# Counting ranks on VectorE with a second masked comparison, and a ReLU wait per step

## The chip, the core and the metric

The kernel runs on one core of one Trainium2 chip. Five engines work side by side, each through its own list of instructions in order: TensorE (matmuls, called PE in the profile, with its weight loads PEld), VectorE (DVE), ScalarE (ACT), GpSimd (POOL), and SyncE (SP), which mostly issues transfers. They wait for each other by semaphores. TensorE writes its results to PSUM, eight banks of 512 float32 values on each of 128 partitions; everything else lies in SBUF. The metric is the device time of one execution in microseconds (us), and each kernel is given by the median of several runs.

## The reference

Two blocks follow each other. The first is a cross attention for 8 batches and 8 heads: 512 rows of `x` (64 wide) read from 32 state rows, and the state rows read from `x`. Both results are put together to 544 rows, and the heads side by side give 512 columns. The second block scores each row, takes the 128 rows with the highest score in each batch, sends them through two layers, and adds the result, weighted by a sigmoid of the score, to those rows alone:

```
xread = softmax(scale * x @ state.T) @ state        # 512 rows
sread = softmax(scale * state @ x.T) @ x            # 32 rows
x2    = concat(xread, sread), heads side by side     # 544 x 512 for each batch
scores[b] = x2[b] @ w_gate
top = the 128 rows with the highest score
h  = relu(x2[b, top] @ w1)                          # 512 -> 1024
ye = h @ w2                                         # 1024 -> 512
out[b] = x2[b];  out[b, top] = x2[b, top] + sigmoid(scores[b, top]) * ye
```

All values are float32.

## The kernel before

The kernel is written as small steps, called pieces, each bound to one engine: `add("PE", "scores", ...)` makes one and names what it must follow and which buffers it takes and uses. Nothing is issued while the pieces are made. At the end `carry_out` (lines 145 to 163) issues them in the order of a list of numbers, `ORDER` (lines 18 to 44). This one list sets the order on every engine and queue, SP's and POOL's among them. An entry such as `663/3/w03` also names the PSUM bank that the piece takes (3), and `w03` puts three warm-up matmuls, whose result nobody reads, into bank 0 ahead of it. If the list doesn't hold every piece's number exactly once, the pieces are issued in the order in which they were made. The text calls a piece by its name and its batch, as in `scores.4`; for the two layers the number is that of the group.

**Attention, one batch at a time (lines 390 to 622).** `x` is loaded in two or four transfers (`load_x`). For batches 0 to 3 TensorE turns it (`turn`) and ScalarE copies it out (`turned`). For batches 4 to 7 a second, rearranged load (`load_x2`, four transfers, one buffer in all) comes in and VectorE turns blocks of it (`blocks`, L405). `scores` (L438) fills two PSUM banks. On VectorE follow `in` (a turn, L457), `max`, `sub`, `sum` and `mult` (the softmax along the state) and `out` (a turn back, L486), with `exp` on ScalarE between them; `smax` and the two `sexp` make the other softmax. `read` (two halves, L549) makes the 512 rows and, in an extra column, their scores by head; `gate` (VectorE, L557) adds these up and `rows` (ScalarE, L553) copies the rows out. For batches 4 to 7 the second softmax's weights are turned by `blocks_a` (VectorE), a transfer to DRAM `a_out` and four transfers back `a_in`; `sread` (L611) then makes the 32 state rows, `srows` scales them. `store_x` and `store_s` write the rows to the output.

**Choice, one batch at a time (lines 664 to 829).** The 544 scores lie in `sc` as five columns: four with 128 partitions, one with 32. `gate_s`, `heads` and `score_s` make the last column. `row` and `row_s` (TensorE) with `row_kept` and `row_s_kept` (ScalarE) spread all scores as one row over every partition, `srow`. A row's rank is the number of rows that beat it. Column `c` of the table `after` masks the places behind the own one, so `win` (L725, five VectorE instructions) compares each score of column `c` with all scores from column `c` on, keeps only the places behind its own, and sums along the row (`over`). It leaves the 0/1 matrix in the buffers `win0` to `win4`. The wins over rows ahead are not computed again: the piece `over` (L751, 15 matmuls with a column of ones) sums those matrices along the other direction. `off` (L757, L758) subtracts the two counts. `oh` (L762) turns the result to a one-hot matrix of 128 slots, `pick` (L778) multiplies it by row numbers and scores (kept by `parts`, POOL, in three bfloat16 parts), `index` makes the row numbers as integers, and `fetch` (POOL) gathers the chosen rows from the output. `below`, `exps`, `plus`, `inverse` and `sigmoid` make the weight.

**Layers, for groups of batches (lines 831 to 928).** The groups are [0], [1, 2], [3, 4], [5, 6] and [7], numbered 0 to 4. `xg` turns the fetched rows, eight pieces `first` (L886) make the first layer, `relu` (L889) copies it out in two or four steps, and `second` (L906; four pieces of two blocks each) makes the second layer for each batch; for batches 6 and 7 it is made in two halves of the columns, `second_h`. `add` or `add_h` (L909) weights and adds, `put` (POOL) scatters the rows to the output. Each `second` piece waits for all `relu` pieces of its group.

Of the kernel before, what the change touches and what calls it, by code (L numbers as in the profile page):

```python
# [15 lines left out]


ORDER = """
0 1 2 4 17 3 6 7 8 9 18 19 10 11 30/5/w08 32/4 34/0/w01 36/1 26/7 31 5 35 27 33 37 12 38/0/w23 113/6 39 13 14 115/5
24/7 40/0 117/4 44 15 114 25 116 45 118 46 28/6 41 16 119/2 62/3 178/4 64/7 180/5 42 120 43 29 63 65 21 23 20 53 487  # L20
182/1 184/6 121/2 267/7 66/0 47 48 122 185 181 268 183 179 67 126 123 49/1 269/4 51/6 50 270 127 128 52 174/4 141/7
54/0 271/5 124 330 55 70 142 125 56 57 272 175 273/7 71/6 58/0 274 129 132 72 59 130 131 176/4 73/5 143/6 75/7 61 177
74 60 76 68 144 69 82 186/4 485/7 133/0 145/6 80 81 79 187 134 188 78 77 191 486 135 136 146 137/0 275/6 140 139 192
193 149 138 280 83/1 208/5/w01 150/2 84 85 151 197 86/3 206/2 152/1 154/0 88 276 189 209 207 87 153 155 281 282 89 22
161 90 210/3 295/2/w01 328/0 297/6 95/7 159 158 160 157 156 333 331 148 147 336 162/1 190 96 329 296 298 211 194 163
195 277 196 278 164 214 97/5 98 102/7 103 99 100 198/0 165/4 215/6 104 199 167 168 335 213 334 279 200 201 101 91
202/0 105 216 283 286 203 284 285 217/5 219/6 226 92 204 106 218 166 220 205 107/7 287/3 239/2 222 221 223 225 224
227/0 108 240 289 290 93 228 229 288 230/5 291/0 299/6 232 292 109 306/4 294 231 300 293 307 337 339 303 340 338 304/6
341/0 305 346 212 332 169 233 315 94 234 308/2 241/6 309 242 347 348 170 313 311 310 314 312 110 243/3 316/6 361 362
342 317 343 318 344 301 302 424 422 426 363 427 425 246/4 249/0 319/1 252/5 250 244 253 247 320 345 245 235 321 111  # L30
349 352 350 431 351 429 428 430 322 364 251 254 353/0 394/5 365/7 354 248 355 356 366 395 357/0 369 370/6 358 371 171
323 112 381 236 372/5 374/4 373 375 359 360 378 380 377 379 376 261/7 255/5 382/2 432/3 256 262 423 490 493 488 368
367 492 491 383 437 384 385/0 263 257 264 258 438 439 237 452 453 387 433 434 496 497 435 172 495 443 494 454 238 388
173 455 396/6 498/2 436 397 398/4 399 456/1 401/6 440 503 259 499 441 504 457 324 505 386 400 442 518 519 460 500 265
589 590 591 459 592 520 489 521 402 444/0 461/5 445 501 446 502 447 404/7 405 407/4 448/0 408 462 506 594 507 509 449
593 508 596 595 472 325 389 406 403 450 451 409 463/5 510/0 465/4 410/6 522/7 464 512 466 513 523 470 511 326 467 468
471 469 526 514/2 473/1 527/7 515 528 474 475 517 516 458 524 587 525 529/0 531/7 530 532 390 535 533 534 537 536
597/4 476/2 411 539/7 327 538 266 391 478 602 540 392 541 412 542/1 603 604 543 477 544 598 617 618 599 600 479 545
260 546 393 480 413 416/2 417 418 551/5 553/4 419 619 588 620 601 552 554 605 420 606 607 608 414 555/7 561/4 558/5
609/0 621/6 556 559 547 611 622 557 612 625 610 613/0 626/6 627 614 481 615 616 482 548 637 421 624 623 562 628/2  # L40
630/1 564/0 629 631 560 563 634 632 633 636 635 565 638/3 566 639 640 549 567/4 641/1 581/3 568 574/6 582 569 575 583
576 584 577 642 645 550 646 580 647 643 578 483 585 648 644 649 669 484 573 579 586 415 662 650/5 651 570 652/0 653
654 655 657/6 658 659 660 656 661 663/3/w03 664 665 666 670/5 671 672 673 571 667 668 572 674 675
"""


# [1 line left out]
def kernel(  # L48
# [10 lines left out]
    nc = tc.nc  # L59
# [24 lines left out]
    def pool(name, bufs, **kw):  # L84
        return ctx.enter_context(tc.tile_pool(name=name, bufs=bufs, **kw))
# [9 lines left out]
    GATES_PE = (0, 2)  # L95
    WIDE = (0, 1, 2, 3)
    ROWS_OUT = ()
    const = pool("const", 1)
    xin = pool("xin", N_X)
    work = pool("work", 1)  # L100
# [121 lines left out]
    wg_h = const.tile([H, D], F32, name="wg_h")  # L222
    wg_T = const.tile([D, H], F32, name="wg_T")
    after = const.tile([128, SP], F32, name="after")
    places = const.tile([128, NC + 1, n_slots], F32, name="places")
    ones = const.tile([128, 1], BF16, name="ones")
    same_n = const.tile([128, Ns], F32, name="same_n")
# [18 lines left out]
    def pool_tables():  # L246

        nc.gpsimd.iota(num[:, 0, :, 0:NC], pattern=[[SP, B], [1, NC]], base=0, channel_multiplier=NC)
        nc.gpsimd.iota(num[:, 0, :, NC], pattern=[[SP, B]], base=S, channel_multiplier=1)
        nc.gpsimd.iota(after, pattern=[[1, SP]], base=0, channel_multiplier=-1, allow_small_or_imprecise_dtypes=True)  # L250
        nc.gpsimd.tensor_scalar(after, after, 0.0, None, op0=ALU.is_gt)

        nc.gpsimd.iota(places, pattern=[[-128, NC + 1], [1, n_slots]], base=0, channel_multiplier=-1,
                       allow_small_or_imprecise_dtypes=True)
        nc.gpsimd.memset(ones, 1.0)

        nc.gpsimd.memset(sc, 0.0)
        for off in offs:  # L260
            nc.gpsimd.memset(off, 0.0)

    def row_numbers():

# [62 lines left out]
    p_w1 = load("SP", "load_w1", lambda: nc.sync.dma_start(out=w1, in_=moe_w1.rearrange("(j p) f -> p j f", p=128)))  # L327
    p_w2 = load("SP", "load_w2", lambda: nc.sync.dma_start(out=w2, in_=moe_w2.rearrange("(j p) m -> p j m", p=128)))
    p_tab = add("POOL", "tables", pool_tables, b=0)
    p_num = add("DVE", "numbers", row_numbers, after=[p_tab], b=0)  # L330
    p_t0 = add("DVE", "twice", lambda: twice(0, N_ST, nc.vector), after=[p_st0], uses=[stb], b=0)
    p_t = add("POOL", "twice", lambda: twice(N_ST, B, nc.gpsimd), after=[p_st], uses=[stb], b=0)
# [331 lines left out]
    def choice(b, tmp, p_sc, p_xt, p_st1):  # L664
# [60 lines left out]
            nc.vector.scalar_tensor_tensor(wins[c].ap[0:n], srow.ap[0:n, f:SP], sc[0:n, b, c:c + 1], after[0:n, 0:SP - f],  # L725
                                           op0=ALU.is_gt, op1=ALU.mult, accum_out=tmp["over"][0:n, c:c + 1])

        p_w = []
        for c in range(NC + 1):
            p_w.append(add("DVE", "win", lambda c=c: win(c), after=[p_r1, p_r2], takes=[wins[c]], uses=[srow], b=b))  # L730

# [22 lines left out]
        def offsets():  # L754
# [76 lines left out]
    def layers(units, number):  # L831
# [41 lines left out]
        p_h = []  # L873
# [23 lines left out]
        for u, lo in zip(units, at):  # L897
# [3 lines left out]
            for k, part in enumerate(parts):  # L901
# [81 lines left out]
```

## Time and profile before

| | |
|---|---|
| median of 3 runs | 204.92 us |
| lowest and highest run | 204.24 and 207.49 us |
| the profiled execution: its own time | 206.27 us |
| the profiled execution: span from first to last instruction | 204.5 us |
| TensorE busy | 192.0 us |
| VectorE busy | 127.7 us |
| ScalarE busy | 77.6 us |
| GpSimd busy | 51.8 us |
| mean granted TensorE clock | 0.981 |

The profile comes from one execution, so that its durations add up to its own time and not to the median. A line of groups names the line, engine, operation, what is written from what, the shape and the number of instructions; then come the total busy time in us, the mean of one in ns, and the idle time before them with what ended it. The granted clock is the share of full speed that TensorE was given. "L751" is line 751 of the kernel.

### The profile page before, as it was taken

Reading aid. Unit: us, or ns where it says so; the run is one execution under the profiler, and the core shown is the slowest. Engines: PE = TensorE matmul, PEld = TensorE weight load, DVE = VectorE, ACT = ScalarE, POOL = GpSimd, SP = SyncE. Lnnn points to the kernel's source line nnn. Section 1 sums busy time; section 2 is a strip of 40 time slices with the busy share of each in tenths; the row PEclk is TensorE's granted clock in tenths of the full one; section 3 lists DMA queues with packets and bytes.
Section 4 is the critical chain, followed back from the end, with each engine's and each line's share of the span. In section 5 each row is a group of like instructions: output and inputs, shape, how many; then the busy total and the mean of one; then the engine's idle time right before and its main releaser. Section 6 shows DMA issues by size and latency. Waiting matters only on the chain.

```text
span 204.5 us, 5844 instructions
## 1 busy us (share of the span) xinstructions
PE 192.0 (94%) x2474; PEld 139.9 (68%) x2474; DVE 127.7 (62%) x293; ACT 77.6 (38%) x178; POOL 51.8 (25%) x147
## 2 busy tenths in 40 slices
PE   7899888899999999899999999799999999999990
PEld 3587666689757688665448887644478886679980
DVE  4279999999966896745899878584764142010100
ACT  2389996682733512371132456312221351011100
POOL 8020030370532307010200004170810032305132
PEclk9999999999999999999999999859999999999999
DMA  6998975059894899979979968085680060101102
GB/s 194 342 273 301 409 274 197 5 113 325 155 305 147 234 263 175 222 127 334 201 135 136 192 159 256 8 260 167 209 193 10 19 258 0 51 0 42 64 26 77
DMA packets 67218, 35.04 MB, mean 171 GB/s; under 512 B 54904, under 2 KB 63096, under 8 KB 66168
## 3 DMA queue, kind: packets, MB, share of 16 engines
q1 hardware_dynamic: 64676, 28.97, 54.8%
q0 software_dynamic: 1312, 4.20, 6.6%
q10 hardware_dynamic: 1204, 1.51, 2.1%
q8 instruction: 19, 0.31, 0.7%
q14 instruction: 7, 0.06, 0.1%
HBM read 21.56 MB, written 13.11 MB: 170 GB/s over the span
## 4 chain that ended last, share of the span: by engine, by line
PE 57%; DVE 8%; DMA 8%; issue 6%; SPq 1%; POOLq 1%; ACT 0%; POOL 0%; DVEq 0%
PE ps L906 24%; PE ps L886 19%; DMA x<-in_x_dram 4%; PE ps L549 4%; DMA xr<-out_dram,idx 2%; PE ps L438 2%; DVE win L725 2%; PE ps L611 2%; PE ps L751 2%; PE ps L690 1%; DVE xT L405 1%; DMA out_dram<-ot,half 1%; PE ps L845 1%; DVE e L457 1%; PE ps L778 1%
## 5 line engine op out<-in xcount | busy, mean ns | idle before, releaser
L906 PE MATMUL ps<-w,hT 128*128 128x512 f32 (+1 forms) x160 | 60.3, 525 | 0.1
L886 PE MATMUL ps<-xg,w 128*128 128x256 f32 (+1 forms) x320 | 59.4, 341 | 0.0
L886 PEld LDWEIGHTS ps<-xg,w 128*128 128x128 f32 x320 | 50.4, 191 | 6.7 <-issue 1.4
L906 PEld LDWEIGHTS ps<-w,hT 128*128 128x128 f32 x160 | 29.7, 193 | 19.4 <-issue 17.2
L553 ACT COPY xs<-ps 128x512 f32<-128x512 f32 x32 | 17.8, 590 | 22.2 <-DVE sc L557 14.1
L909 DVE SCALAR_TENSOR_TENSOR ot<-ps,z,xr 128x512 f32<-128x512 f32 (+1 forms) x10 | 6.4, 639 | 26.6 <-PE ps L906 20.2
L725 DVE SCALAR_TENSOR_TENSOR win<-srow,sc,after 128x160 bf16<-128x160 f32 (+4 forms) x40 | 18.4, 511 | 5.4 <-ACT srow L716 5.4
L549 PE MATMUL ps<-st_v,eT 32*64 32x65 f32 (+1 forms) x768 | 16.6, 246 | 3.1 <-ACT xs L553 1.4
L549 PEld LDWEIGHTS ps<-st_v,eT 32*64 32x64 f32 (+1 forms) x768 | 14.3, 149 | 7.0 <-issue 4.6
L656 POOL DMA_INDIRECT xr<-out_dram,idx x8 | 8.5, 1066 | 38.6 <-DVE idx L782 25.1
L889 ACT ACTIVATE hT<-ps 128x512 f32<-128x512 f32 x16 | 9.4, 602 | 18.2 <-PE ps L886 18.2
L735 POOL CAST aux<-sc 128x5 bf16<-128x5 f32 x8 | 2.9, 356 | 46.7 <-DVE sc L557 32.6
L474 ACT ACTIVATE e<-e 128x1024 f32<-128x1024 f32 x8 | 8.5, 1064 | 15.8 <-DVE e L471 15.8
L496 ACT ACTIVATE a<-ps,nm 128x512 f32<-128x512 f32 x14 | 9.5, 689 | 12.9 <-DVE nm L492 9.2
L405 DVE STREAM_TRANSPOSE xT<-x 128x512 f32<-128x512 f32 x16 | 10.5, 683 | 2.8 <-DMA x<-in_x_dram 2.8
L478 DVE TENSOR_REDUCE sm<-e 128x32 f32<-128x1024 f32 x8 | 9.7, 1208 | 2.6 <-ACT e L474 2.6
L848 ACT COPY xg<-ps 128x512 f32<-128x512 f32 x8 | 4.6, 586 | 15.7 <-PE ps L845 15.7
L401 PE MATMUL ps<-ident,xf 128*128 128x128 f32 x64 | 9.8, 289 | 0.5 <-DMA xf<-in_x_dram 0.5
L438 PE MATMUL ps<-xT,st_T 64*32 64x256 f32 x256 | 9.8, 413 | 0.0
L483 DVE TENSOR_TENSOR e<-e,sm 128x1024 f32<-128x1024 f32 x8 | 9.7, 1207 | 0.0
L418 ACT COPY xT<-ps 128x512 f32<-128x512 f32 x14 | 7.9, 592 | 4.5 <-PE ps L401 4.5
L492 DVE TENSOR_REDUCE nm<-ps 128x2 f32<-128x1024 f32 x7 | 8.5, 1213 | 1.7 <-PE ps L693 1.0
(107 smaller groups left out, 242.6 us busy)
## 6 DMA issues: line engine op xcount, KB each, us to landing
xf<-in_x_dram SPq DMA_DIRECT2D x14, 512.0 KB, 7.1
out_dram<-xs SPq DMA_DIRECT2D x7, 1024.0 KB
w<-in_moe_w_dram SPq DMA_DIRECT2D x2, 2048.0 KB, 14.7
x<-in_x_dram SPq DMA_DIRECT2D x16, 256.0 KB, 8.6
a_d<-spare SPq DMA_DIRECT2D x4, 512.0 KB
aT<-a_d SPq DMA_DIRECT2D x16, 128.0 KB, 3.4
out_dram<-xs ACTq DMA_DIRECT2D x1, 1024.0 KB
xf<-in_x_dram SPq DMA_DIRECT2D x3, 256.0 KB
```

What stands on the lines that cost most here:

```text
L401: nc.tensor.transpose(v[:, k, r], xf[b].ap[:, 2 * pair + k, 2 * r:2 * r + 2].rearrange("p w d -> p (w d)"), ident)
L405: nc.vector.transpose(out=t.ap.rearrange("p k r t -> p r k t"), in_=x2[b].ap[:, :, 2 * pair:2 * pair + 2].rearrange("p r k s d -> p r k (s ...
L438: nc.tensor.matmul(view_s(False)[Ns * q:Ns * (q + 1), w, g], st_T[half, b, g, Ns * q:Ns * (q + 1)], xT[2 * g + q // 2].ap[half, q % 2].rea ...
L478: nc.vector.reduce_sum(out=sm, in_=e.ap, axis=AX.X)
L483: nc.vector.tensor_tensor(out=e.ap, in0=e.ap, in1=tmp["sm"].to_broadcast([128, 32, Ns]), op=ALU.mult)
L496: nc.scalar.activation(out=a.ap[:, g], in_=view_s()[:, :, g], func=AF.Exp, bias=tmp["nm"][:, g:g + 1], accum_out=tmp["ss"][:, g:g + 1])
L549: nc.tensor.matmul(view(o)[t, q, c - c0, g], eT.ap[r, c % 2, g, c // 2, t], st_v[r, b, g], start=True, stop=True)
L553: nc.scalar.copy(out=xs.ap[:, c].rearrange("p (g q m) -> p g q m", g=2, q=4), in_=view(o)[:, :, c - c0, :, 0:D].rearrange("p q g m -> p g ...
L725: nc.vector.scalar_tensor_tensor(wins[c].ap[0:n], srow.ap[0:n, f:SP], sc[0:n, b, c:c + 1], after[0:n, 0:SP - f], op0=ALU.is_gt, op1=ALU.mu ...
L886: nc.tensor.matmul(o, w(j), i[:, :, j] if n == 256 else i[:, 0, j], start=(j == 0), stop=(j == ND - 1))
L889: nc.scalar.activation(out=hT.ap[:, f0:f0 + nf, 0:n], in_=ph.ap.rearrange("p (f s) -> p f s", f=nf)[:, :, 0:n], func=AF.Relu)
L906: nc.tensor.matmul(py.ap[0:m, part], hT.ap[:, f, lo:lo + m], w2[:, f, part], start=(f == 0), stop=(f == NF - 1))
```

## The change

There are two edits, and a new order.

For batches 3 to 7 (`FULL`) a second set of five comparisons, `low`, is made on VectorE. It compares each score of column `c` with all scores up to the end of that column, takes "less than", masks by a new table `before`, and sums along the row (`under`). `before` holds ones for all columns ahead and, for the own column, zero at the own place and behind. GpSimd makes it once, with three operations. The piece `over` with its 15 matmuls is not made for these batches, and `off` subtracts `under` from `over`, both in SBUF. All five `low` write their unneeded 0/1 matrix into the buffer `win0`. Batches 0 to 2 are as before.

In the layers, a `second` piece for the blocks `f0` and `f0 + 1` waits for the ReLU pieces up to the one that makes these blocks, and no more for the later ones.

`ORDER` is replaced as a whole: 697 numbers in place of 676. The order of pieces on all engines and queues, the banks and the warm-ups (30 in place of 17) differ. On TensorE the three warm-ups before the last `second_h.4` are gone, `state_T.0` is ahead of the last two `turn.0`, both `xg.1` stand behind `row_s.3`, and two `second_h.3` stand ahead of the last `first.3`. On VectorE `out.4` stands ahead of the four `blocks.5`, and the `low` are interleaved with the `win`. On POOL `before` stands behind `below.0` and ahead of `parts.1`, and `fetch.1` behind `parts.2`. On SP `a_out.4` has three `load_x2.5` and a `load_x.5` ahead of it, and `a_in.4` one `load_x2.5` and `store_s.3` between.

```diff
+    FULL = (3, 4, 5, 6, 7)
...
+    before = const.tile([128, S + 128], BF16, name="before") if FULL else None
...
+    def pool_before():
+
+        nc.gpsimd.memset(before[:, 0:S], 1.0)
+        nc.gpsimd.tensor_tensor(out=before[:, S:S + 128], in0=after[:, 0:128], in1=ident, op=ALU.add)
+        nc.gpsimd.tensor_scalar(before[:, S:S + 128], before[:, S:S + 128], -1.0, 1.0, op0=ALU.mult, op1=ALU.add)
...
+    p_bef = add("POOL", "before", pool_before, after=[p_tab], b=1) if FULL else None
...
-        p_w = []
+        def low(c):
+            if "under" not in tmp:
+                tmp["under"] = small.tile([128, NC + 1], F32, name="under")
+            n, f = rows[c], first[c]
+            nc.vector.scalar_tensor_tensor(unders[c].ap[0:n, 0:f + n], srow.ap[0:n, 0:f + n], sc[0:n, b, c:c + 1], before[0:n, S - f:S + n],
+                                           op0=ALU.is_lt, op1=ALU.mult, accum_out=tmp["under"][0:n, c:c + 1])
+
+        p_w, p_l = [], []
+        full = b in FULL
+        unders = [Buf(R_WIN[0]) for c in range(NC + 1)]
+        for c in range(NC + 1 if full else 0):
+            p_l.append(add("DVE", "low", lambda c=c: low(c), after=[p_r1, p_r2, p_bef], takes=[unders[c]], uses=[srow], b=b))
...
+        def offsets_full():
+            nc.vector.tensor_tensor(out=offs[b % 2][:, 0:NC], in0=tmp["over"][:, 0:NC], in1=tmp["under"][:, 0:NC], op=ALU.subtract)
+            nc.vector.tensor_tensor(out=offs[b % 2][0:Ns, NC:NC + 1], in0=tmp["over"][0:Ns, NC:NC + 1], in1=tmp["under"][0:Ns, NC:NC + 1],
+                                    op=ALU.subtract)
...
-        p = add("PE", "over", wins_over, after=p_w, takes=[ps3], uses=wins, b=b)
-        p = add("DVE", "off", offsets, after=[p, chosen_by.get(b - 2)], uses=[ps3], b=b)
+        if full:
+            p = add("DVE", "off", offsets_full, after=p_w + p_l + [chosen_by.get(b - 2)], b=b)
+        else:
+            p = add("PE", "over", wins_over, after=p_w, takes=[ps3], uses=wins, b=b)
+            p = add("DVE", "off", offsets, after=[p, chosen_by.get(b - 2)], uses=[ps3], b=b)
...
-                    p = add("PE", "second_h" if n_parts > 1 else "second", lambda f0=f0, go=second_layer: go(f0), after=p_h + [p_w2, p], takes=[] if f0 else [py], uses=[hT] + ([py] if f0 else []), b=number)
+                    p = add("PE", "second_h" if n_parts > 1 else "second", lambda f0=f0, go=second_layer: go(f0), after=p_h[0:f0 // nf + 1] + [p_w2, p], takes=[] if f0 else [py], uses=[hT] + ([py] if f0 else []), b=number)
```

More of the change, by code (lines that the diff above doesn't have):

```diff
@@ L18 @@
 ORDER = """
[L19 to L43, printed above, removed]
+0 1 2 4 17 3 6 7 8 9 19 20 10 11 31/7/w08 33/6 27/0 35/3 37/2 5 28 32 36 34 38 12 39/0/w03 114/2 40 13 14 116/6 25/5
@@ new lines @@
+41/0 45 15 117 26 115 46 47 42 43 16 118/7 29/6 120/2 179/3 181/5 63/4 183/0 65/1 119 121 44 66 180 64 182 24 22 21 54
+500 122/1/w23 185/3 268/7 48 49 123 127 184 269 186 30 67/4 50/5 270/3 52/6 68 51 271 128 129 55/0/w07 175/5 272/4
+142/7 124 125 133 71 56 53 126 57 58 273 176 143 72/6 59/0 274/4 275 335 130 73 60 131 132 74/5 144/6 76/7 177/4 75 62
+77 178 61 69 145 70 83 187/4/w51 134/0 498/7 146/6 79 81 82 188 135 78 192 80 136 137 499 147 138/0 276/6 141 140 193
+194 150 189 139 281 84/2 151/1 85 86 152 198 153/3 207/2 87/5/w01 155/4 209/1 89 154 88 208 156 210 282 283 90 23 91
@@ new lines @@
+18 162 190 161 157 160 159 158 277 211/0/w04 333/3 298/2 296/1 96/4 163/7 212 191 92 97 299 334 297 195 196 278 197
+279 164 215 165 103/6 98/5 104 99 100 199/0 101 105 166/4 216/7 200 338 341 336 149 337 214 339 148 340 280 201 202
+102 167 203/0 106 284 217 285 204 168 286 218/5 220/4 93 170 227 206 219 221 205 108/7 288/0 224 223 225 222 226 228/5
+109 107 290 171 291 287 229 230 289 231/6 292/1 300/0 233 232 294 295 301 342 343 94 344 293 345 304 110 307/5 305/1
+346/2 306 351 347 213 169 234 95 321 172 235 309/6 240/1 242/0 308 241 243 310 352 353 111 247/4 244/0 253/2 254 248
@@ new lines @@
+245 314 348 366 316 311 367 319 318 312 315 317 313 320 349 322 323 302 433 431 434 436 368 435 303 369 324/5 250/6
+350 325 246 255 249 354 326 355 356 251 358/1 370/5 112 437 359 440 357 438 360 361 371 252 236 362/1/w01 374 375/7
+363 376 439 327 113 328 237 391 403/0 377/5 379/6 365 378 380 404 364 262/7 441/2 256/5 263 264 432 501 503 373 504
+372 506 505 389 238 382 388 387 390 383 381 384 386 385 446 392 393 394/6 257 265 258 259 329 447 448 461 396 462 442
+173 443 444 509 510 507 508 463 397 330 174 239 502 464 405/3 445 406 395 511/0 410/6 407/3 408 465/4 449 331 516 512
@@ new lines @@
+452 450 451 517 518 409 466 260 531 532 606 607 609 533 608 534 453/0 411 413/4 513 454 514 266 469 455 456 515 457/0
+470/5 416/7 414 417 519 520 458 612 471 521 613 522 611 610 332 398 261 486 459 460 415 412 399 418 472/5 474/4 523/0
+419/6 535/7 473 475 525 526 536 479 481 478 484 485 483 524 476 480 539 527/0 540/4/w41 528 477 482 541 487 488 530
+529 467 468 538 604 537 542/7 544/5/w51 543 545 614/2 489/4 420 421 422 556 400 267 552 553 551 546 555 549 554 548
+547 550 557 491 558 619 559/7 490 560 620 621 561 634 401 635 615 625 616 617 423 492 562 402 493 563 425/1 426 427
@@ new lines @@
+568/7 570/2 428 636 605 637 569 571 618 494 622 623 429 624 572/7 575/5 573 578/4 626/0 638/6 576 628 564 629 574 639
+627 642 630/0 643/7 579 644 631 632 633 577 495 565 424 659 640 641 645/2 647/6 581/3 598/5 591/0 582 584/7 646 648
+580 583 496 651 649 655 653 654 656 652 650 657 658 660 661 566 662/2 585 599 592 600 593 601 586 594 663 567 666 667
+497 668 664 669 595 602 665 670 430 590 683 597 603 596 690 671/4 672 587 678/3 673/4 679 674 675 676 680 681 677 682
+684/4 685 686 687 691/2 692 693 694 588 688 689 589 695 696
```

## The prediction

> **What bounds the kernel now.** I read the page first, its busy shares and its chain of waits:
>
> ```profile
> PE 192.0 (94%) x2474; PEld 139.9 (68%) x2474; DVE 127.7 (62%) x293; ACT 77.6 (38%) x178; POOL 51.8 (25%) x147
> PE 57%; DVE 8%; DMA 8%; issue 6%; SPq 1%; POOLq 1%; ACT 0%; POOL 0%; DVEq 0%
> ```
>
> TensorE is busy 94% and holds 57% of the chain. The stretches of 10 us say when: VectorE is at 9.6 to 9.9 of 10 from 20 to 50 us, TensorE at 9.8 or more in most stretches from 40 on. So the start, up to 42.9 us where batch 0's rows are turned (`xg.0`), hangs on VectorE; behind it runs a queue of TensorE work until 199.4 (192.35 + 7.07), then an addition, a scatter and its landing to 204.5.
>
> Next the groups by form, for what is removed (L751) and repeated (L725):
>
> ```profile
> L751 PE MATMUL ps<-ones,win 128*128 128x1 bf16 x80 | 3.2, 164 | 0.7 <-DVE sc L557 0.6
> L725 DVE SCALAR_TENSOR_TENSOR win<-srow,sc,after 128x544 bf16<-128x544 f32 x8 | 6.2, 775 | 0.0
> L725 DVE SCALAR_TENSOR_TENSOR win<-srow,sc,after 128x160 bf16<-128x160 f32 x8 | 3.1, 387 | 0.7 <-ACT srow L716 0.7
> ```
>
> Last TensorE's timeline where the change acts (start, length, what, idle before), and the granted clock (TensorE busy, weight loads, VectorE, ScalarE, GpSimd, then the clock):
>
> ```profile
> 85.18 0.91 PE L549 MATMUL ps<-st_v,eT 32*64 32x65 f32 x64 [0.58 <-DVE eT L486]
> 130.72 0.80 PE L549 MATMUL ps<-st_v,eT 32*64 32x65 f32 x51 [1.20 <-issue]
> 169.26 0.68 PE L751 MATMUL ps<-ones,win 128*128 128x1 bf16 x15
> 184.56 7.31 PE L886 MATMUL ps<-xg,w 128*128 128x128 f32 x64
> 191.71 0.81 PE L161 MATMUL ps<-ident 128*128 128x512 bf16 x3
> 192.35 7.07 PE L906 MATMUL ps<-w,hT 128*128 128x256 f32 x32
> ```
> ```profile
> 129.00:130.00 1.00, 0.52 (x31) 0.29 (x19) 0.61 (x5) 0.52 (x2) 0.00 (x0) 1.00 0.00 0
> 130.00:131.00 1.00, 0.28 (x32) 0.28 (x33) 0.15 (x2) 0.00 (x0) 0.00 (x0) 1.00 0.00 0
> 132.00:133.00 1.00, 1.00 (x9) 0.97 (x7) 0.57 (x4) 0.85 (x2) 0.31 (x2) 0.50 0.00 0
> 137.00:138.00 1.00, 1.00 (x3) 0.47 (x2) 0.75 (x1) 0.15 (x1) 1.00 (x2) 0.50 0.75 266
> ```
>
> The reader should see: the counting is 15 tiny matmuls in a full queue; the last layer's second half waits for a ReLU behind three warm-ups; and one gap of 1.2 us among small matmuls is followed by a half clock from about 131.9 to 138.4.
>
> The profiled execution took 206.27 us, 1.35 above the median of 204.92. The half clock explains it: 6.5 us at half do 3.25 us of work, so it cost 3.2. Without it the profile would be 203.0. I work out a difference and set it on the median.
>
> **The change part by part.**
>
> *The 15 matmuls leave (batches 3 to 7).* In the chain the batch-7 group takes 0.51 us, other groups 0.51 to 0.63. 5 x 0.51 = **2.55 us** off TensorE's queue.
>
> *Ten comparisons instead of five.* Starts in the timeline follow one another by 0.137 us plus width/960 (160 wide: 0.31, 288: 0.44, 544: 0.71). The new widths are 128, 256, 384, 512 and, on 32 partitions, 544: 0.27 + 0.40 + 0.54 + 0.67 + 0.70 = **2.59 us** a batch, 12.9 in all, VectorE 127.7 to 140.6. The five share one scratch buffer with `win0`; if each waited for the one before it to end (a dependent pair starts about 0.1 later than an independent one) it would be 3.1, at the other end 2.59. They are interleaved with `win`: I take 2.59. The subtraction keeps its two instructions of 0.14; PSUM's copy is gone, gain under 0.1, taken as nothing.
>
> Whether this hides is a race in each batch between VectorE and what the new order puts before `pick` on TensorE. The path is row copies 0.7, comparisons 4.77 (2.18 + 2.59), subtraction 0.15, one-hot 0.85, hop 0.2: 6.7 us, plus VectorE steps placed between.
> - Batch 3: VectorE from the scores of batch 4 to `oh.3`: maximum and turn 2.3, comparisons 4.8, maximum 1.1, turned blocks 1.3, subtraction 1.1, the rest 1.0 = 11.8. TensorE: `xg.1` 0.9, `second.0` 1.9, six `first.1` at 1.83 = 13.8. Hidden by 2. `out.4` is due after 16.1 (the rest of the softmax follows), `read.4` after 17.6: hidden by 1.4, and since `out.4` no longer stands behind the blocks of batch 5, the 0.58 wait at 85.18 goes.
> - Batch 4: 6.7 + 1.1 (maximum of 5) = 7.8; TensorE has four `second.1` (7.4) and the scores (1.0) = 8.4. Hidden.
> - Batch 5, counted from `row_s.5`: `oh.5` at 7.2; TensorE reads, waits for `score_s.6` behind the comparisons, and does the scores of 7 by 7.5. The small steps heads, row and row_s (0.92) take 1.8: **+0.9**, two warm-ups included.
> - Batch 6: comparisons start when VectorE is free at 7.25, `oh.6` at 13.2; TensorE arrives at 13.2: **+0.2**.
> - Batch 7: 6.7; TensorE two `first.3`, two `second_h.3`, one `second.3` = 7.3. Hidden. `xg.4` follows 9.1 later; the fetch takes 2.9 to its start (171.96 to 174.87) and 3.3 to 6.1 to land: just hidden.
>
> *A page against it.* When GpSimd's cast (L735) met VectorE's two-input multiplication at 27.97 it took 1.05 us for its usual 0.20, ending with it. The Trainium skill, "SBUF — State Buffer", section "SBUF: two separate sides", generalises: a VectorE instruction with two SBUF inputs and a GpSimd one that reads SBUF exclude each other for a whole instruction. Each new comparison is such a one. By the row 0.8 a meeting, by the rule up to 0.7 for each of four GpSimd steps, 2.8 a batch. Both fall on `parts.6`, done by about 10 against a pick at 13.2: nothing.
>
> *The table `before` on GpSimd.* Its three operations are not in the trace: memset 512 wide (0.20 for 128 wide), addition and scale 128 wide (544 wide took 1.63, so 0.4 each): 1.0 to 1.7, to 3 behind VectorE. It runs near 45 us, where GpSimd sat idle 8.1 us before the fetch of batch 1. Behind it wait `parts.1`, `plus.0`, `below.1`, `parts.2` and that fetch, which now stands behind `index.1` and `parts.2`: start about 55.8 (`index.1` at 54.3 behind the softmax of 3, then `parts.2`) for 53.4, landing about 61; both `xg.1` moved behind the scores of 4, near 66. Nothing; without that cover 2.4.
>
> *ReLU.* `second_h.4` runs its first two steps (1.77 us) without the last ReLU, which ends 0.85 after the last `first.4`. The gap between 191.87 (184.56 + 7.31) and 192.35 goes: **-0.5**. It could be 0.3 to 0.7; nothing is queued behind, since a wait leaves.
>
> *The new order.* On SP, `a_out.4` follows VectorE's turned blocks, now 1.5 later (6.3 after the scores of 4), and its read-back one load (minus 1.5) and one small store (plus 0.6) otherwise. Before, the state read started 14.7 after `a_out.4` was issued. So 20.1 after the scores against 18.6 wanted: 1.5. Two waits before, at 86.5 and 87.9 (0.45 together), fall inside. **+1.0**, bounds -0.4 and 2.0; I take it nearer the trace than the walk, as SP's issues stretched from 0.6 to 2.6 us when the queues were full. The loads of 6 keep their place before the second half of batch 4's stores; landing near 101 suffices. Warm-ups: 27 instead of 14 before `xg.0`, where TensorE idles about 5 us and VectorE rules: nothing, at most 1.5. A third late one before `read.4`: 0 to 0.2, inside that wait. At the start `state_T.0` goes ahead (-0.4) and `gate.0` on VectorE ahead of `gates.4` (+0.3): nothing, between -0.4 and 0.5.
>
> *Sum.* -2.55 - 0.5 - 0.58 - 0.45 + 0.9 + 0.2 + 1.0 = **-2.0**. 206.3 becomes 204.3 with a half clock of the same length; 204.92 becomes **202.9**.
>
> *The clock.* The skill's "TensorE: Matmul & The Clock Gate", section "Part 1: The HAM clock gate", lets the clock fall after an idle window of about 3.4 us; the trace shows it at 0.50 after a gap of 1.2. By the rule the new gaps (0.9 at most) cost nothing; by the row a sparse stretch costs 3.2. The row decides: between `sread.6` and the scores of 7 TensorE is sparse for 5.4 us before, 3.7 after, with warm-ups. I expect the risk to be somewhat smaller and put 0.3 of it into the forecast: **202.6**.
>
> **The rivals.**
> 1. *TensorE stays the bound, some gain given back* (0.62): 202.6, its own range 200.9 to 204.6.
> 2. *All waits covered and no half clock* (0.23): -4.1 and the median's share of the clock (204.92 less 203.0, of which about 0.6 stays as scatter: -1.3) give 199.5. For: TensorE's list is shorter and every pick had slack on paper. Against: sums of 13.2 against 13.2.
> 3. *VectorE sets the pace for batches 5 and 6* (0.15): `score_s.6` and `oh.6` stand behind ten comparisons each. From about 1.2 us of added wait among the small steps the clock halves, as at 130.72. -2.0 + 2.0 of waits + 3.2 for a second half clock - 0.6 already counted = +2.6: 207.5. For: VectorE is at 8.4 and 8.5 of 10 in the stretches from 110 to 130 already. Against: it idles 1.2 to 2.0 before four of the subtractions (L757), waiting for the matmuls that leave.
> 4. *The written order is not used*: the list must number every step; 676 - 5 + 25 + 1 = 697, and it runs to 696. Excluded.
>
> **How the numbers follow.** About 2% is what a measurement here can tell from no change: under 200.8 or over 209.0. Case 2 gives 0.22 of faster and case 1's low end 0.04; slower has a third of case 3, 0.05. The range 199.5 to 206.2 leaves out a tenth below and a tenth above.
>
> **What would show it.** No L751 for batches 3 to 7; VectorE near 140; `out.4` ahead of `read.4`; no gap before the last 32 matmuls; TensorE's waits at `sread.4`, `row_s.6` and `pick.6` near 1.0, 0.9 and 0.2. I am wrong if comparisons cost over 3 us a batch, if a half clock appears or leaves, or if transfers for batches 5 and 6 come later.

## The result, and the profile after

| | before | after |
|---|---|---|
| median | 205.37 us (20 runs) | 202.45 us (20 runs) |
| lowest and highest run | 203.95 and 208.10 us | 201.05 and 204.11 us |
| ratio of after to before | | 0.9865, interval 0.9836 to 0.9895 |
| profiled execution: its time, its span | 206.27, 204.5 us | 203.17, 201.4 us |
| mean granted TensorE clock in it | 0.981 | 0.999 |

The kernel became faster by 1.35%, which is less than the 2% that a measurement is taken to tell from no change; the interval leaves out 1. Runs more than 1.5% above the fastest of their kernel count as slow, and the ratios, here and below, leave them out. The forecast was 202.6, that is 2.3 below the 204.92 of three runs; with 20 runs before stands at 205.37, and the change is 2.9. So the number was met, but with some luck: the base was 0.45 low, and three terms of the sum were wrong, which cancel only in part (see the part on why).

The page of the changed kernel, its busy times and its chain of waits:

```profile
PE 189.4 (94%) x2412; PEld 138.3 (69%) x2412; DVE 141.5 (70%) x343; ACT 77.6 (39%) x178; POOL 52.2 (26%) x150
PEclk9999999999999999999999999999999999999999
PE 56%; DVE 14%; DMA 5%; issue 4%; ACT 2%; POOL 1%; POOLq 1%; DVEq 0%; ACTq 0%
```

TensorE lost 2.6 us of work and still holds 56% of the chain. VectorE gained 13.8 us of work, and its share of the chain rose from 8% to 14%: some of the comparisons now lie on the path, at least those ahead of `pick.6`; where the chain goes through VectorE from 91 to 107 us, it hangs on a releaser that the profile names wrongly (told of below). The clock line has no dip.

The groups by form of the changed kernel (line, engine, operation, written from read, number; then busy us, mean ns, idle before):

```profile
L742 DVE SCALAR_TENSOR_TENSOR win<-srow,sc,before 32x544 bf16<-32x544 f32 x5 | 3.9, 772 | 0.1
L742 DVE SCALAR_TENSOR_TENSOR win<-srow,sc,before 128x512 bf16<-128x512 f32 x5 | 3.7, 739 | 1.8 <-ACT srow L724 1.8
L772 PE MATMUL ps<-ones,win 128*128 128x1 bf16 x30 | 1.2, 164 | 0.4 <-DVE sc L567 0.4
```

Five comparisons a batch in five batches are there, and of the counting matmuls only those of batches 0 to 2 (30 in place of 80).

TensorE's timeline of the changed kernel where it waits or where a wait was foreseen (start, length, what, and in brackets the idle time before it):

```profile
66.63 0.66 PE L874 MATMUL ps<-ident,xr 128*128 128x128 f32 x4
68.77 0.63 PE L874 MATMUL ps<-ident,xr 128*128 128x128 f32 x4 [1.49 <-DMA xr<-out_dram,idx]
...
81.31 0.35 PE L807 MATMUL ps<-aux,oh 128*128 128x5 bf16 x5
...
85.24 1.04 PE L559 MATMUL ps<-st_v,eT 32*64 32x65 f32 x49
86.68 0.44 PE L559 MATMUL ps<-st_v,eT 32*64 32x65 f32 x15 [0.40 <-issue]
87.06 1.10 PE L621 MATMUL ps<-xf,aT 128*32 128x64 f32 x64
...
99.06 0.36 PE L807 MATMUL ps<-aux,oh 128*128 128x5 bf16 x5
...
107.55 0.63 PE L874 MATMUL ps<-ident,xr 128*128 128x128 f32 x4 [1.07 <-DVE sm L488]
...
141.74 0.36 PE L807 MATMUL ps<-aux,oh 128*128 128x5 bf16 x5 [0.33 <-DVE oh L788]
...
171.21 0.35 PE L807 MATMUL ps<-aux,oh 128*128 128x5 bf16 x5
...
182.36 7.31 PE L915 MATMUL ps<-xg,w 128*128 128x128 f32 x64
189.51 7.07 PE L935 MATMUL ps<-w,hT 128*128 128x256 f32 x32
```

L807 is `pick`: those of batches 3, 4 and 7 (81.31, 99.06, 171.21) don't wait. `read.4` (85.24) and `sread.4` (87.06) no longer wait for another engine. The last 32 matmuls follow the first layer directly (182.36 + 7.31 = 189.67; starts overlap a little). New are the waits before the second `xg.1` (1.49) and the second `xg.2` (1.07), for which nothing was forecast. For the second one the profile names an addition of the softmax (L488), which ended 0.12 ahead of it but which this turn doesn't need; what it needs is `fetch` of batch 4, issued at 100.24 and landed 7.2 us later.

By stage, from the starts on TensorE in the profiled executions. The version `relu_old`, told of below, has before's order and ran its profile at clock 0.995, so that it stands in for a before at full clock:

| from one start to the next | before | `relu_old` | after | after less before | forecast |
|---|---|---|---|---|---|
| first `xg.0` to first `first.1` | 26.63 | 27.94 | 27.94 | +1.3 | 0 |
| to first `first.2` | 37.75 | 37.61 | 38.18 | +0.4 | -1.05 |
| to first `first.3` | 44.02 | 41.03 | 40.75 | -3.3 | +0.1 at an equal clock |
| to `xg.4` | 31.10 | 31.13 | 30.33 | -0.8 | -0.5 |
| to the last 32 matmuls | 9.94 | 9.30 | 9.30 | -0.6 | -0.5 |
| to the end of the span | 12.15 | 12.14 | 11.89 | -0.3 | 0 |

The forecast column sorts the terms of the prediction's sum by the stage that they belong to (its -2.0 in all). In the third stage the half clock of before's profile is worth 44.02 - 41.03 = 3.0, less 0.2 for a shorter gap: 2.8. From the third stage on the change gains what was forecast or somewhat more; in the first two it does not, and there the two new waits lie. The first stage differs between executions too: in the old order `relu_old` needs 27.94 there, by small waits for other engines (0.18, 0.52 and 0.32), and `before_warm` 27.24. The profiled execution of before, at 26.63, is the shortest of the three, so the +1.3 is the most that this stage can have lost.

### The profile page after: what moved, and what is told of

Its sections match the earlier page's. It is cut to its first block, busy times and chain, and to the rows that moved or that the text cites. A ratio compares the mean times of both kernels' runs of the same rounds, so it can differ in the third digit from the quotient of the medians.

```text
span 201.4 us, 5778 instructions
## 1 busy us (share of the span) xinstructions
PE 189.4 (94%) x2412; PEld 138.3 (69%) x2412; DVE 141.5 (70%) x343; ACT 77.6 (39%) x178; POOL 52.2 (26%) x150
## 3 DMA queue, kind: packets, MB, share of 16 engines
q1 hardware_dynamic: 64676, 28.97, 55.8%
## 4 chain that ended last, share of the span: by engine, by line
PE 56%; DVE 14%; DMA 5%; issue 4%; ACT 2%; POOL 1%; POOLq 1%; DVEq 0%; ACTq 0%
PE ps L915 29%; PE ps L935 15%; PE ps L559 5%; DMA xr<-out_dram,idx 5%; DVE win L742 4%; DVE win L735 3%; PE ps L874 2%; DVE xT L415 2%; PE ps L621 1%; POOL out_dram L666 1%; PE ps L700 1%; DVE oh L788 1%; PE ps L807 1%; DVE spare L583 1%; PE ps L772 1%
## 5 line engine op out<-in xcount | busy, mean ns | idle before, releaser
L935 PE MATMUL ps<-w,hT 128*128 128x512 f32 (+1 forms) x160 | 58.7, 513 | 0.0
L666 POOL DMA_INDIRECT xr<-out_dram,idx x8 | 9.6, 1194 | 44.1 <-DVE idx L811 21.2
L735 DVE SCALAR_TENSOR_TENSOR win<-srow,sc,after 128x416 bf16<-128x416 f32 (+4 forms) x40 | 18.9, 506 | 1.9 <-ACT srow L726 1.7
L559 PE MATMUL ps<-st_v,eT 32*64 32x65 f32 (+1 forms) x768 | 18.0, 247 | 1.5 <-issue 0.8
L559 PEld LDWEIGHTS ps<-st_v,eT 32*64 32x64 f32 (+1 forms) x768 | 15.2, 149 | 6.0 <-issue 2.9
L742 DVE SCALAR_TENSOR_TENSOR win<-srow,sc,before 128x512 bf16<-128x512 f32 (+4 forms) x25 | 14.7, 588 | 4.9 <-ACT srow L724 4.5
L163 PE MATMUL ps<-ident 128*128 128x512 bf16 x30 | 9.8, 447 | 1.3 <-POOL ident masks.py:199 1.3
L756 POOL CAST aux<-sc 128x5 bf16<-128x5 f32 x8 | 2.4, 306 | 31.4 <-DVE sc L689 17.8
L488 DVE TENSOR_REDUCE sm<-e 128x32 f32<-128x1024 f32 x8 | 9.6, 1204 | 0.9 <-ACT e L484 0.8
```

The source lines that it names most:

```text
L163: nc.tensor.matmul(banks[:, 512 * bank:512 * (bank + 1)], same_b[:, 0:128], same_b.unsqueeze(1).to_broadcast([128, 2, 256]), start=True, s ...
L488: nc.vector.reduce_sum(out=sm, in_=e.ap, axis=AX.X)
L559: nc.tensor.matmul(view(o)[t, q, c - c0, g], eT.ap[r, c % 2, g, c // 2, t], st_v[r, b, g], start=True, stop=True)
L666: st = nc.gpsimd.indirect_dma_start(**kw)
L742: nc.vector.scalar_tensor_tensor(unders[c].ap[0:n, 0:f + n], srow.ap[0:n, 0:f + n], sc[0:n, b, c:c + 1], before[0:n, S - f:S + n], op0=ALU ...
L935: nc.tensor.matmul(py.ap[0:m, part], hT.ap[:, f, lo:lo + m], w2[:, f, part], start=(f == 0), stop=(f == NF - 1))
```

## The experiments

Each version ran beside before on one of two chips. Before's median there was 205.36 (`count_old`, `relu_old`, `fetch_late`, `no_warm6`) and 205.40 (the others), for 205.37 beside the changed kernel, so that the versions are set against its 202.45 as they are.

### The comparisons in the old order

`count_old` keeps before's order and the old ReLU wait. Only the counting changes: each `low` stands behind a `win`, and `over` is gone for batches 3 to 7. VectorE, batch 3:

```diff
 smax.4
 win.3
+low.3
...
 blocks_a.4
 in.4
 off.3
```

> Order of before; only the counting is changed (low behind each win for batches 3 to 7, over gone, the table made on GpSimd behind below.0); every second step still waits for all ReLUs and the three last warm-ups stay. Theory (TensorE's queue is the bound, VectorE's extra work mostly hidden): 2.55 us leave the queue and about 1 us comes back as waits for the one-hot of batches 4 to 6, so 0.993 of before. Rival (VectorE sets the pace of this order): the ten comparisons come late in every batch, 5 x 2.6 less the 1.2 to 2.0 it idled before, so 1.00 to 1.02 of before.

Measured: 211.81 us (210.81 to 212.87, 6 runs), ratio 1.0304, interval 1.0241 to 1.0367. My theory (203.9) fell by eight microseconds, and the rival's 1.00 to 1.02 was too low as well. TensorE's timeline of this version, its four long waits:

```profile
76.94 3.06 PE L915 MATMUL ps<-xg,w 128*128 128x256 f32 x8 [2.99 <-DVE off L784]
...
135.78 0.27 PE L686 MATMUL ps<-part_s,same_n 128*32 128x1 f32 x2 [1.51 <-DVE scr L679]
...
145.32 0.36 PE L807 MATMUL ps<-aux,oh 128*128 128x5 bf16 x5 [2.18 <-DVE oh L788]
...
178.27 0.36 PE L807 MATMUL ps<-aux,oh 128*128 128x5 bf16 x5 [1.55 <-DVE oh L788]
```

VectorE's timeline of this version just before the first of them:

```profile
73.83 0.60 DVE L742 SCALAR_TENSOR_TENSOR win<-srow,sc,before 128x384 bf16<-128x384 f32 x1
...
74.37 1.29 DVE L583 STREAM_TRANSPOSE spare<-a 128x512 f32<-128x512 f32 x2
75.59 1.20 DVE L467 STREAM_TRANSPOSE e<-ps 128x1024 f32<-128x1024 f32 x1
76.72 0.11 DVE L783 TENSOR_TENSOR off<-over,under 128x4 f32<-128x4 f32 x1
```

The wait of 2.99 is before a first-layer matmul that needs no rank at all. What ends just ahead of it on VectorE is `in.4` (L467, 75.59 + 1.20 = 76.79), the turn that reads batch 4's scores out of PSUM; it stands behind all ten comparisons here. The profile names the small subtraction beside it, but the list settles it: this matmul is the first of the third `first.1`, which takes bank 0, and that is where `scores.4` lies. The other readers of these scores, `smax.4` and both `sexp.4`, had ended by 70.9. In the changed kernel `in.4` stands ahead of the first `low`. The four waits are 8.2 us, and the clock line shows what they cost besides:

```profile
PEclk9999999999999988999999999888899999999999
```

So the comparisons are no gain by themselves. In the old order, placed like this, they are 6.4 us dearer than the matmuls that they replace (211.81 against 205.36 for before on the same chip).

### The ReLU wait alone

`relu_old` is before with the new wait, and without the three warm-ups ahead of the last `second_h.4`:

```diff
-... after=p_h + [p_w2, p], ...
+... after=p_h[0:f0 // nf + 1] + [p_w2, p], ...
```

> Order of before; only the ReLU wait is changed and the three warm-ups ahead of the last second layer are left out. Theory: the gap of 0.48 us ahead of the last 32 matmuls closes, 0.997 to 0.998 of before, and nothing else moves. Rival (the wait is hidden or another one stands behind it): 1.000, the gap in the timeline still there.

Measured: 204.94 us (202.68 to 207.83, 22 runs), ratio 0.9947, interval 0.9910 to 0.9985. Taking only runs with a granted clock of 0.990 or more, medians 203.96 (10 runs) against 204.40 (15 runs of before): 0.44 us. The interval of the ratio allows for 0.3 to 1.8. TensorE's timeline of this version:

```profile
182.52 7.31 PE L886 MATMUL ps<-xg,w 128*128 128x128 f32 x64
189.66 7.07 PE L906 MATMUL ps<-w,hT 128*128 128x256 f32 x32
```

From `xg.4` to the last 32 matmuls it takes 9.30, as after, for 9.94 before, so 0.64. The step is worth 0.4 to 0.6 us by these two counts, as forecast. It does nothing about the clock: 12 of 22 runs lie below 0.990.

### The new order with the old counting

`order_over` has the changed kernel's order and ReLU wait, and puts the 15 matmuls back for batches 3 to 7, one TensorE step ahead of each subtraction (for instance `read.6`, `over.5`, `heads.6`):

```diff
-    FULL = (3, 4, 5, 6, 7)
+    FULL = ()
```

> The new order and the new ReLU wait, but the ranks of batches 3 to 7 counted as before: no low, no table, and the 15 matmuls of over one TensorE step ahead of the subtraction. Theory (each part of the queue counts): the matmuls come back, 2.55 to 3.0 us above the changed kernel, 0.999 to 1.002 of before. Rival (the gain is the order's and the clock's; the counting itself gives nothing): within 0.6 us of the changed kernel, 0.984 to 0.990 of before.

Measured: 204.57 us (203.72 to 207.39, 22 runs), ratio 0.9965, interval 0.9945 to 0.9986. TensorE's timeline of this version at the fetch, and one of the groups that came back:

```profile
68.77 0.63 PE L873 MATMUL ps<-ident,xr 128*128 128x128 f32 x4 [1.53 <-DMA xr<-out_dram,idx]
...
170.08 0.68 PE L771 MATMUL ps<-ones,win 128*128 128x1 bf16 x15
```

The result lies between my two expectations (2.55 to 3.0 us above the changed kernel, or within 0.6). Two things follow. The counting is worth 204.57 - 202.45 = 2.1 us in the new order (2.55 of matmuls by the forecast, less what VectorE makes TensorE wait), where it cost 6.4 in the old one. And the wait of 1.5 at the second `xg.1` is there without a single new comparison: it comes with the order, and the table on GpSimd isn't its cause either, since this version doesn't make it. Order and ReLU wait together are worth 0.8 of before's median, most of it the ReLU step and a half clock that now comes seldom: 20 of 22 runs lie at 0.990 or more, and their median of 204.50 is 0.36 below that of before's 17 such runs on this chip (204.86). The order saves next to nothing by itself; it is what makes room for the comparisons.

### How much room is left on VectorE

`low_twice` is the changed kernel with each `low` issued twice, the second time with the same result, so 12.9 us more VectorE work by the prediction's price of one set:

```diff
             nc.vector.scalar_tensor_tensor(unders[c].ap[0:n, 0:f + n], ... accum_out=tmp["under"][0:n, c:c + 1])
+            nc.vector.scalar_tensor_tensor(unders[c].ap[0:n, 0:f + n], ... accum_out=tmp["under"][0:n, c:c + 1])
```

> The changed kernel with each low issued twice, 2.6 us more of VectorE in each of batches 3 to 7. Theory (the new order hides one set with 0.6 to 2 us to spare in batches 3, 4 and 7 and with nothing to spare in 5 and 6): 0.6 to 1.2 + 2.0 + 2.6 + 2.6 + 2.0 = about 10 us above the changed kernel, 1.03 to 1.04 of before, the waits standing ahead of the picks. Rival (VectorE has room, 141 of 201 us): under 4 us above the changed kernel.

Measured: 217.86 us (216.55 to 222.26, 8 runs), ratio 1.0596, interval 1.0555 to 1.0637: 15.4 us above after, for 14.6 us more of VectorE (156.1 busy). That is over the 10 that I expected. TensorE's timeline of this version at the picks of batches 4, 6 and 7, and its clock:

```profile
103.77 0.38 PE L809 MATMUL ps<-aux,oh 128*128 128x5 bf16 x5 [3.15 <-DVE oh L790]
...
154.41 0.39 PE L809 MATMUL ps<-aux,oh 128*128 128x5 bf16 x5 [2.06 <-DVE oh L790]
...
188.55 0.38 PE L809 MATMUL ps<-aux,oh 128*128 128x5 bf16 x5 [2.97 <-DVE oh L790]
```
```profile
PEclk9999999999997999998599999969699999699999
```

This profile is of one of the three longest executions, of 222.04 us: 18.9 above the profiled one of the changed kernel, at a mean clock of 0.951, where the other runs lie between 0.951 and 0.982. Its waits for VectorE behind `xg.0` are 11.7 us, for 0.3 in the changed kernel, so that here about 3 of the 14.6 found cover; most of what is left of the 18.9 goes with the half clock, which takes up 20.5 us of this execution. How the 15.4 of the median divides is not shown. The changed kernel thus uses nearly all the room that VectorE has in these batches, in this order.

### The two fetches

`fetch_late` is the changed kernel with the second `xg.1` one TensorE step later, and the second `xg.2` behind `scores.6`; their copies on ScalarE move with them:

```diff
 TensorE: xg.1
-xg.1
 second.0
+xg.1
 first.1
...
-xg.2
 scores.6
+xg.2
 ScalarE: xg_kept.1
-xg_kept.1
 row_s_kept.3
 sexp.4
 sexp.4
+xg_kept.1
```

> The changed kernel with its two waits for fetched rows covered: the second turn of rows of batch 2 (xg.1, with its copy) one second-layer step later, that of batch 4 (xg.2, with its copy) behind the scores of batch 6. Theory (these waits of 1.49 and 1.07 us are what the new order gave back): 2.0 to 2.5 us below the changed kernel, 0.975 of before. Rival (VectorE or the transfers set the pace there, so another wait takes their place): within 0.5 us of the changed kernel, 0.984 to 0.987 of before.

Measured: 201.96 us (201.44 to 202.43, 6 runs), ratio 0.9834, interval 0.9776 to 0.9892. That is next to the rival's 0.984 to 0.987, and the theory's 0.975 lies outside the interval. From the changed kernel (0.9865) it can't be told apart. TensorE's timeline of this version:

```profile
70.52 10.63 PE L915 MATMUL ps<-xg,w 128*128 128x256 f32 x48 [1.58 <-ACT xg L877]
...
108.45 5.45 PE L915 MATMUL ps<-xg,w 128*128 128x256 f32 x24 [0.67 <-ACT xg L877]
```

Both waits moved one step down, from the turn to the layer that reads its copy, since the copy of `xg.1` now stands behind both `sexp.4`, and nothing is left between the second `xg.2` and the layer that would cover its copy.

`both_late` puts the copy between the two `sexp.4`, and takes the two warm-ups out of batch 6:

```diff
 row_s_kept.3
 sexp.4
+xg_kept.1
 sexp.4
-xg_kept.1
...
-540/4/w41 (heads.6)   544/5/w51 (row_s.6)
+540/4                 544/5
```

> The changed kernel with the second xg.1 one second-layer step later and its copy between the two exponentials of batch 4 (in the run before, the copy stood behind both and TensorE waited for it instead), the second xg.2 behind the scores of batch 6, and without the two warm-ups of batch 6. Theory (the waits for fetched rows can be covered): 1.4 to 2.0 us below the changed kernel, 0.977 to 0.980 of before. Rival (the next wait takes over): 0.983 of before, as each of the two edits alone.

Measured: 201.02 us (200.78 to 201.83, 6 runs), ratio 0.9800, interval 0.9770 to 0.9830, apart from the changed kernel's (0.9836 to 0.9895). It has the lowest median of all, 1.4 us below after; from `fetch_late` and `no_warm6` its interval doesn't separate it. TensorE's timeline of this version:

```profile
70.00 10.63 PE L915 MATMUL ps<-xg,w 128*128 128x256 f32 x48 [0.81 <-ACT xg L877]
...
86.73 1.10 PE L621 MATMUL ps<-xf,aT 128*32 128x64 f32 x64 [0.40 <-DMA aT<-a_d]
...
108.31 5.45 PE L915 MATMUL ps<-xg,w 128*128 128x256 f32 x24 [0.68 <-ACT xg L877]
```

From `xg.0` to `first.1` it takes 27.30, after 27.94. The new line is the one at 86.73: once TensorE comes earlier out of the fetch, `sread.4` waits for its own transfer, which the fetch had covered.

### The warm-ups of batch 6

`no_warm6` is the changed kernel without the two warm-ups:

```diff
-540/4/w41 (heads.6)   544/5/w51 (row_s.6)
+540/4                 544/5
```

> The changed kernel without the two warm-ups ahead of heads.6 and row_s.6. Theory (they keep the clock up in the sparse stretch of batch 6): the half clock of about 6.5 us comes back in many runs, 1 to 3 us above the changed kernel, 0.992 to 1.000 of before. Rival (a gap under 1 us doesn't drop the clock[...]): 0 to 0.4 us below the changed kernel, granted clock 0.99 or more.

Measured: 201.86 us (201.30 to 202.17, 6 runs), ratio 0.9832, interval 0.9775 to 0.9889; the clock was 0.993 or more in every run. TensorE's timeline of this version:

```profile
131.53 0.22 PE L686 MATMUL ps<-part_s,same_n 128*32 128x1 f32 x2 [0.38 <-DVE scr L679]
...
132.67 0.24 PE L703 MATMUL ps<-ident,sc 32*128 32x32 f32 x1 [0.33 <-DVE sc L689]
```

Where the warm-ups stood there are now waits of the same length: from the start of the last `read.6` to that of the scores of 7 it takes 2.60, and 2.59 with warm-ups. The half clock did not come back in six runs, so the theory fell: waits of 0.3 to 0.4 did not bring it here. The median is 0.6 below the changed kernel's, but this place gave none of it, and the intervals overlap; in its profile the start is 0.6 earlier and the wait at the second `xg.2` is missing. I give no gain to this edit.

### Where the half clock of before comes from

`before_warm` is before with seven warm-ups in the sparse stretch of batch 6:

```diff
-473/1 (over.5)        527/7 (heads.6)
+473/1/w14             527/7/w73
```

> The kernel before with seven more warm-ups in the sparse stretch of batch 6: four ahead of over.5, three ahead of heads.6. Theory (the half clock comes from that stretch): runs with a granted clock under 0.990 disappear, where 12 of 27 runs of before had one; 7 x 0.22 = 1.5 us are added to the clean time of 204.4, so 205.5 to 206.0 with little scatter, 1.003 of before. Rival (the half clock comes at random or from elsewhere): the same share of runs under 0.990, median near 206.9, 1.007.

Measured: 205.76 us (204.40 to 206.74, 22 runs), ratio 1.0011, interval 0.9991 to 1.0032. The clock was 0.990 or more in 21 of 22 runs, and in 17 of 43 of before on the same chip. TensorE's timeline of this version, and two stretches of 2 us (TensorE, weight loads, VectorE, ScalarE, GpSimd, clock, share of the transfers, GB/s):

```profile
131.83 0.80 PE L549 MATMUL ps<-st_v,eT 32*64 32x65 f32 x51 [1.25 <-issue]
132.56 1.04 PE L161 MATMUL ps<-ident 128*128 128x512 bf16 x4
```
```profile
134.00:136.00 2.00, 2.00 (x28) 1.15 (x35) 0.91 (x4) 0.31 (x1) 0.65 (x2) 1.00 0.65 262
136.00:138.00 2.00, 2.00 (x40) 1.01 (x25) 1.79 (x6) 0.46 (x3) 1.70 (x4) 1.00 1.07 262
```

The gap of 1.25 us is still there, and the clock behind it stays at 1.00, where before it was 0.50. This profile alone doesn't show that the warm-ups did it, since `relu_old` has the gap too, no warm-up behind it, and a clock of 1.00:

```profile
131.41 0.80 PE L549 MATMUL ps<-st_v,eT 32*64 32x65 f32 x51 [0.97 <-issue]
```

What shows it is the count of runs: 21 of 22 for 17 of 43. The one run below 0.990 is the profiled one, and its half clock lies elsewhere, from 38.58 to 41.99, behind no gap above 0.65 in the 5 us ahead. So this stretch of batch 6 is where most of before's half clock comes from, and the warm-ups keep it away; a gap of a given length neither brings it for sure nor is needed for it. Seven warm-ups cost about what the half clock does on average, so nothing is won by them.

## Why the prediction was right, and where it was not

**TensorE stays the bound.** Right: it is busy 94% of the span, as before, and the likeliest case and its 202.6 hold. Two rivals fell: not all waits were covered (199.5), and VectorE does not set the pace (207.5) in the new order. In the old order it does, with 211.8. The fourth, that the order isn't used, is out as well: the timeline has both `xg.1` (66.63, 68.77) next to each other, and 30 warm-ups run (L163), which only the list asks for.

**The 15 matmuls, -2.55.** Right as far as the runs tell: `order_over` gives 2.1 for the whole counting, and the wait at `pick.6`, which the comparisons bring, takes 0.33 off.

**Ten comparisons for five, 2.59 a batch.** Near: 13.8 us in five batches are 2.76 each. Of the choice between 2.59 and 3.1 for the shared scratch buffer the truth lies between: a `low` starts about 0.1 later right behind another instruction that writes `win0`, and the order puts only some of them in a row.

**The races in each batch.** Right in batches 3, 4 and 7, with no wait at their picks, and at `pick.6` (0.33 for 0.2). For batch 5 the small steps from `heads.6` to the scores of 7 take 1.75 us (132.93 to 134.68) for 1.8 forecast, so +0.8 for +0.9. In these steps the warm-ups only fill the waits. That the paper slack was real but thin is what `low_twice` shows.

**The ReLU wait, -0.5.** Right: 0.44 by the runs of `relu_old`, 0.64 by the starts in the profile.

**`out.4` and the two waits behind it, -0.58 and -0.45.** The first went. In the place of the others is a gap of 0.40 inside one group of matmuls, at 86.68, that no semaphore explains. It costs more than its length: from the start of `read.4` to that of the next piece it takes 1.82 (85.24 to 87.06), for 0.84 in before (85.18 to 86.02).

**`xg.1`: "Nothing; without that cover 2.4".** This is the step that failed. I followed the fetch of batch 1 and let it land near 61 with both `xg.1` near 66. But the layer's group is batches 1 and 2, and the second `xg.1` needs the fetch of batch 2, which follows on the same queue. The chain of the changed kernel, in order of time (start, length, what):

```profile
63.33 0.41 issue
63.74 4.90 DMA xr<-out_dram,idx
68.64 0.14 issue
68.77 0.63 PE ps L874 x4
```

In the old order this fetch landed in time. GpSimd's and TensorE's timelines of before:

```profile
63.17 1.07 POOL L656 DMA_INDIRECT xr<-out_dram,idx  x1 [4.73 <-DVE sc L557]
67.32 0.66 PE L845 MATMUL ps<-ident,xr 128*128 128x128 f32 x4
```

It landed after 3.6 us, at 66.8, half a microsecond ahead of the turn. In the new order it goes out 0.6 later and takes 4.9, and TensorE comes at 67.28, no earlier than before: the wait of 1.49 is the difference. The later start is within what executions of the old order show (63.66 in `relu_old`, 63.70 in `before_warm`); the longer way is not. The fetch of batch 2 took 3.4 to 3.6 us in these three profiles of the old order (4.4 in `count_old`), and 4.9 to 5.2 in all six of the new one, `order_over` among them.

The first fetch was off as well, though its turn did not wait: it was forecast to start at 55.8, went out at 60.13 (53.39 in before) and landed at 63.8, ahead of 66.63. A fetch gathers its rows from the output, so it must follow their store, which the forecast didn't count. SP's timeline of the changed kernel, and below it that of before, where fewer loads stand ahead, have the store of batch 1 5.7 us apart:

```profile
51.36 3.38 SPq L655 DMA_DIRECT2D out_dram<-xs  x1
```
```profile
45.67 0.49 SPq L645 DMA_DIRECT2D out_dram<-xs  x1
```

That the store is what the fetch waited for is my reading: its row numbers were ready at 53.9, and the profile names an instruction of batch 2 that it doesn't need.

The second `xg.2` is of the same kind: in the changed kernel its fetch took 7.2 us, for 3.8 in before, while the transfers ran at a share of 1.03 (100 to 110 us). The prediction leaves it out. This wait stands in the profile of the changed kernel, and not in those of `order_over` and `no_warm6`, where that fetch took 5.4 and 6.0.

**SP's order at `sread.4`, +1.0.** Wrong by itself: 0. The walk set the read-back at 20.1 us after the scores of 4, against a wanted 18.6. But TensorE reached `sread.4` only 21.6 after the scores (65.43 to 87.06). Of these 3.0 us more, 1.49 are the wait for the fetch and 0.40 the gap inside `read.4`. The two waits lie one behind the other, and the longer came first. When `both_late` takes part of the fetch's wait away, 0.40 of the forecast wait shows up.

**What the sum was worth.** A term of +1.0 that was not paid stood in for two of +1.49 and +1.07 that were not seen, and the -0.45 was used up by gaps inside groups: by the starts two of them cost 1.9 in after, and one 1.5 in before. With the measured terms the sum is -2.55 - 0.64 - 0.58 + 0.83 + 0.33 + 1.49 + 1.07 = -0.05, not -2.0. That fits the two profiled executions (-0.2 by the stages at an equal clock), but the medians moved by 2.0 to 2.4 at full clock. About 1.1 of the rest is the wait at the second `xg.2`, which other executions of the new order don't have, and 0.6 to 1.3 may be the short first stage of before's profile (26.63 for 27.24 and 27.94). So the errors made up for each other only in part; that the sum met the median is luck for the rest.

**The table on GpSimd.** Right: hidden. Its three operations, in GpSimd's timeline of the changed kernel, and the step behind them:

```profile
43.34 0.53 POOL L268 MEMSET before<- 128x512 bf16 x1
43.82 0.45 POOL L269 TENSOR_TENSOR before<-after,ident 128x128 bf16<-128x128 f32 x1
44.37 0.30 POOL L270 TENSOR_SCALAR before<-before 128x128 bf16<-128x128 bf16 x1
...
44.90 1.12 POOL L757 TENSOR_TENSOR rest<-sc,aux 128x5 f32<-128x5 f32 x1
```

1.3 us for 1.0 to 1.7. The last line is a step of usually 0.20 (66.04) that took 1.12 beside VectorE, as the row of before had it, and nothing waits for it. At `pick.6` the one-hot of VectorE came last and not GpSimd, so the rule on shared ports that was weighed there cost nothing, as forecast. Nor did the additional early warm-ups: `xg.0` starts at 43.01 for 42.91, and waits 0.54 for its own fetch.

**The clock, -0.3.** Right in sign, small in size. Before's half clock lasted from 131.89 to 138.71, 6.8 us and not 6.5. The rule of the Trainium skill ("TensorE: Matmul & The Clock Gate", "Part 1: The HAM clock gate") asks for an idle window of about 3.4 us. No such window lies ahead of the last matmul in either profile, and the mean clock was below 0.990 in 12 of 27 runs of before on one chip and 26 of 43 on the other, in none of 20 of after (lowest 0.991; a half clock of 3.4 us takes only 0.008 off the mean, so that one of this length may hide there). The measurement decides against the idle window, and for the stretch of batch 6 as the place (`before_warm`). It doesn't bear out the row's gap of 1.2 as a threshold: longer gaps of 1.49 (after) and 1.55 (`count_old`, 178.27) left the clock at 1.00. What the threshold is, no run shows. The medians of before with and without those runs are 205.36 and 204.40 on the first chip, 205.40 and 204.86 on the second: the half clock is worth 0.5 to 1.0 of the median. Against runs at full clock the change is worth 2.0 to 2.4, for -2.0 forecast.

**What stays open.** Why the fetches take longer in the new order, what brings the gaps inside groups of equal matmuls, and what exactly brings the half clock. With before's third stage at 41.03 the stage table gives only -0.2 for the two profiled executions, and the split above of what the medians have beyond that rests on three or four single executions. `relu_old` loses 1.3 in the first stage without the new fetch waits, so no single stage of these profiles can be trusted to 1 us.

## What to carry to other kernels

When work is moved to an engine with idle time, ask first what stands behind it on that engine: the same ten comparisons cost 6.4 us in one order and saved 2.1 in another; the longest of the waits (2.99) came from a turn out of PSUM that stood behind them. Follow every transfer that a moved step needs, and not only the first of its group, back to the store whose rows it reads. Waits on one queue do not add up: the first to be paid covers the next, so the terms of such a sum can be wrong in pairs, and removing one wait shows another.

## What the runs showed of the hardware

- The granted clock fell to half for 6.83 us in before (131.89 to 138.71) and for 3.41 us each time in `count_old` (from 77.65, 135.68 and 145.92) and `before_warm` (from 38.58). The longest gap ahead does not decide it: it fell behind gaps of 1.20 (before) and of at most 0.65 (`before_warm`, 38.58), and stayed at 1.00 behind 0.97 (`relu_old`), 1.25 (`before_warm`), 1.49 (after) and 1.55 (`count_old`).
- Gaps of 0.4 to 1.25 us lie inside one group of equal matmuls, with no semaphore ahead of them (`issue`): 1.20 in before, 1.25 in `before_warm`, 0.97 in `relu_old`, 0.40 and 0.38 in after. Their cause is open.
- A fetch of 128 rows landed 3.6 us (batch 2), 3.8 (batch 4) and 5.0 (batch 1) after its issue in before, and 4.9, 7.2 and 3.7 for the same batches in after. The 7.2 fell into 10 us with the transfers at a share of 1.03; what sets the others is open.
